# Attention with a feed-forward: float32 loads on the hardware queue and casts on the chip, in place of casting loads from GpSimd's queue

## The chip, the cores and the metric

The kernel runs on one core of a Trainium2 chip. The metric is the device time of one execution in microseconds. The core has a matrix engine (TensorE, PE in the profile; its weight loads are listed apart as PEld), a vector engine (VectorE, DVE), an activation engine (ScalarE, ACT), GpSimd (POOL) and a sequencer that only issues transfers (SyncE, SP). Each works through its own list of instructions in order and waits on semaphores; transfers run on 16 DMA engines.

## What is computed

Windowed attention, followed by a feed-forward layer with a squared ReLU:

```python
# q, k, v: 4 batches, 8 heads, 768 positions, 64 values, float32; n_global = 8, n_local = 96
scores = q @ k.T / sqrt(64)                     # per batch and head
keep = (col < n_global) | ((row - col >= 0) & (row - col < n_local))
dist = where(col < n_global and not local, n_local, abs(row - col))
a = softmax(where(keep, scores - slope[head] * dist, -1e9))
x = (a @ v), heads side by side                 # 3072 x 512
h = maximum(x @ w_in, 0)                        # w_in: 512 x 2048
out = (h * h) @ w_out                           # w_out: 2048 x 512, out float32
```

## The kernel before

**Tiles and stages.** The work is cut into eight half-batches (`hb`, 384 positions each, three blocks of 128). For each, `attention(hb)` makes a list of small jobs over four pairs of heads: `prep` turns q and k of a pair so that the head dimension lies on the partitions, `score` multiplies and applies exp and the mask (two groups), `attend` multiplies with v and divides by the row sums, `to_x` turns the result into `xt`. `ffn(hb)` makes 28 jobs: 16 of `first` (x times w_in, then ReLU and square) and 12 of `second` (times w_out, out). All matrix work is in float16 with float32 sums.

**Order.** TensorE's order is the order in which the jobs are called, fixed by `manual_schedule`. Attention of half-batch 0 stands alone; then `merge` weaves attention of `hb + 1` between the jobs of `ffn(hb)`, about one by one, from the second job on. The other engines' order is made by the framework's scheduler, and each then keeps it.

**Loads.** `load(b, half, h0, h1)` takes the q, k and v tiles of a half-batch, three of 128 positions each. All loads are issued by GpSimd, whose queue also casts float32 in memory to float16 in SBUF. The first half-batch is loaded in two groups of four heads, then come `w_in` in four pieces, half-batch 1, `w_out` in four pieces, half-batch 2, and later half-batches two ahead of use. Outputs go out on SP's queue.

**Around v and k.** A query block looks at its own 128 columns and at the block before. For the block before, copies are kept in which the first 32 rows are replaced by the first 32 of the sequence, where the global columns are: `kb` for k (L172, L173) and `vb` for v (L156 to L159), both made by VectorE. The column of ones that follows v's 64 values gives the row sums.

**Buffers.** `ps_att` (tag `att`) has two PSUM buffers, used in turn by the turned q and k (`trp`), by `av` and by `trx`. `ps_big` has three, used by the scores, by `first` and by `second`. `phat_p` has three of each of its tiles (`ex` and `phat`). `qk_p` has two buffers of q and k turned, `kb`, `v` and `vb`, one for each of two batches.

Of the kernel before, what the change touches and what calls it, by code (L numbers as in the profile page):

```python
# [32 lines left out]
def kernel(  # L33
# [11 lines left out]
    nc = tc.nc  # L45
# [17 lines left out]

    const = ctx.enter_context(tc.tile_pool(name="const", bufs=1))
    stage_p = ctx.enter_context(tc.tile_pool(name="stage", bufs=2))
    qk_p = ctx.enter_context(tc.tile_pool(name="qkp", bufs=2))
    phat_p = ctx.enter_context(tc.tile_pool(name="phat", bufs=3))
    tm_p = ctx.enter_context(tc.tile_pool(name="tm", bufs=3))
    h_p = ctx.enter_context(tc.tile_pool(name="hp", bufs=2))
    y_p = ctx.enter_context(tc.tile_pool(name="yp", bufs=2))  # L70
# [5 lines left out]
    distc = const.tile([P, 2 * P], FP32, name="distc")  # L76
    pidx = const.tile([P, 1], FP32, name="pidx")
    ident = const.tile([P, P], FP16, name="ident")
    local = const.tile([P, 2 * P], FP16, name="local")
    ge0 = const.tile([P, 2 * P], FP16, name="ge0")  # L80
    isg = const.tile([P, 1], FP32, name="isg")
# [9 lines left out]
    def fill_index():  # L91
        nc.gpsimd.iota(dist, pattern=[[1, 2 * P]], base=0, channel_multiplier=-1,
                       allow_small_or_imprecise_dtypes=True)
        nc.gpsimd.iota(pidx, pattern=[[0, 1]], base=0, channel_multiplier=1,
                       allow_small_or_imprecise_dtypes=True)
        nc.vector.tensor_scalar(out=ident, in0=dist[:, 0:P], scalar1=0.0, scalar2=None,
                                op0=ALU.is_equal)

    def fill_masks():
# [30 lines left out]
        bt.sk = [None, None]  # L130
        batches.append(bt)

    def load(b, half, h0, h1):
        bt = batches[b]
        if half == 0 and h0 == 0:
# [5 lines left out]
        if h0 == 0:  # L141
            bt.sq[half] = stage_p.tile([P, HT, H, D], FP16, name="sq", tag="sq")
            bt.sk[half] = stage_p.tile([P, HT, H, D], FP16, name="sk", tag="sk")
        rows = slice(half * HALF, (half + 1) * HALF)
        for src, dst in ((q, bt.sq[half]), (k, bt.sk[half]),
                         (v, bt.v[:, half * HT:(half + 1) * HT, :, 0:D])):
            for t in range(HT):
                r0 = half * HALF + t * P
                nc.gpsimd.dma_start(  # L149
                    out=dst[:, t, h0:h1, :],  # L150
                    in_=src[b, h0:h1, r0:r0 + P, :].rearrange("h p d -> p h d"))

    def fix_v(b, half):
        bt = batches[b]
# [5 lines left out]

    def prep(b, half, a):
        bt = batches[b]
        trp = ps_att.tile([P, 2, HT, P], FP16, name="trp", tag="att")
        for i, st in enumerate((bt.sq[half], bt.sk[half])):
            for t in range(HT):
                nc.tensor.transpose(out=trp[:, i, t, :], in_=st[:, t, 2 * a:2 * a + 2, :],  # L166
                                    identity=ident)
        nc.scalar.copy(out=bt.qk[:, :, a, half * HALF:(half + 1) * HALF],  # L168
                       in_=trp.rearrange("p i t c -> p i (t c)"))
# [143 lines left out]

    fill_index()
    for h0 in range(0, H, 4):
        load(0, 0, h0, h0 + 4)
    fill_masks()
    for c in range(4):
        load_w_in(c)
    load(0, 1, 0, H)  # L320
    for c in range(4):
        load_w_out(c)
    load(1, 0, 0, H)
    with tc.manual_schedule(engines={PE}):
        for job in attention(0):
            job()
        for hb in range(NHB):
            if 1 <= hb and hb + 2 < NHB:
                load((hb + 2) // 2, hb % 2, 0, H)
# [39 lines left out]
```

## Time and profile before

| | before |
|---|---|
| time of the runs (two) | 261.21 and 261.45 us, median 261.33 |
| span of the profiled execution | 258.2 us (its total time is not listed) |
| TensorE busy | 227.6 us, 88% of the span |
| VectorE, ScalarE, GpSimd busy | 139.6, 135.0, 75.9 us |
| GpSimd's queue (casting loads) | 79248 packets, 13.64 MB |
| SP's queue (outputs) | 3328 packets, 6.29 MB |

How to read it: the span runs from the first to the last instruction of the profiled execution; the time of a run lies a little above it. "Busy" is time in which an engine executes, summed over the span. Issuing a load counts as an instruction of GpSimd. A row such as `L272 PE MATMUL hps<-xt,w_in_sb` names the line of the program, the engine, the operation, the tile written and the tiles read. "idle before <-" tells what ended the engine's idle time before that instruction. The megabytes of GpSimd's queue are those written, in float16; twice as many are read.

### The profile page before, as it was taken

The page shows a single profiled execution, that of the slowest core. Times are in us where ns is not written, and L with a number is a line of the kernel's source. Part 1 is how long each engine was busy: PE and PEld are TensorE (multiplying, and loading weights), DVE is VectorE, ACT ScalarE, POOL GpSimd, SP SyncE. Part 2 cuts the span into 40 slices and gives each one's busy share as a digit, 9 for nine tenths or more (in the row PEclk, how much of TensorE's full clock was granted, in tenths as well). Part 3 has the DMA queues.
Part 4 walks back from the last instruction along what each step waited for, and adds up shares of the span by engine and source line. Part 5 has one row for each costly group of instructions (what it writes and reads, how often), then busy time and mean ns, then how long its engine had stood idle before and what let it go on. Part 6 is the DMA issues. An engine that isn't in the chain of part 4 may idle for free.

```text
span 258.2 us, 4590 instructions
## 1 busy us (share of the span) xinstructions
PE 227.6 (88%) x1888; PEld 125.0 (48%) x1888; DVE 139.6 (54%) x331; ACT 135.0 (52%) x201; POOL 75.9 (29%) x95
## 2 busy tenths in 40 slices
PE   1428769928999999999699999999999999999994
PEld 0216345514555555645455555655654565555541
DVE  8558237454778336746676436843675346543411
ACT  5436359601297329941587329831984179623600
POOL 8996573696207000528008000700000000000000
PEclk9999999985999999999999999999999999999999
DMA  6999999999909930499909630792100210003003
GB/s 44 87 116 205 169 179 208 156 153 109 209 1 63 62 121 3 29 96 76 169 3 84 41 122 3 50 76 81 43 0 0 85 41 3 0 5 119 0 3 122
DMA packets 82597, 20.22 MB, mean 78 GB/s; under 512 B 75408, under 2 KB 79504, under 8 KB 82576
## 3 DMA queue, kind: packets, MB, share of 16 engines
q0 software_dynamic: 79248, 13.64, 71.0%
q1 hardware_dynamic: 3328, 6.29, 6.6%
q8 instruction: 15, 0.25, 0.4%
q14 instruction: 6, 0.05, 0.1%
HBM read 27.26 MB, written 6.29 MB: 130 GB/s over the span
## 4 chain that ended last, share of the span: by engine, by line
PE 54%; DMA 17%; ACT 11%; POOL 11%; DVE 3%; issue 2%; DVEq 0%; POOLq 0%
PE yps L284 27%; PE hps L272 19%; DMA v<-in_v_dram 8%; POOL v L149 5%; DMA w_out_sb<-in_moe_w_out_dram 5%; DMA w_in_sb<-in_moe_w_in_dram 5%; ACT hr L276 4%; ACT ex L205 4%; PE av L220 3%; ACT qk L168 3%; PE sp L201 3%; POOL sq L149 2%; POOL sk L149 2%; PE trx L239 1%; POOL w_out_sb L310 1%
## 5 line engine op out<-in xcount | busy, mean ns | idle before, releaser
L272 PE MATMUL hps<-xt,w_in_sb 128*128 128x384 f16 x512 | 98.5, 329 | 2.6 <-DVE y L289 1.9
L276 ACT ACTIVATE hr<-hps 128x768 f16<-128x768 f32 x64 | 52.8, 825 | 43.9 <-PE hps L272 43.0
L272 PEld LDWEIGHTS <-w_in_sb 128*128 128x128 f16 x512 | 45.9, 98 | 31.4 <-issue 3.2
L205 ACT ACTIVATE ex<-sp 128x768 f16<-128x768 f32 x64 | 47.8, 779 | 8.9 <-PE sp L201 8.8
L149 POOL DMA_DIRECT2D sq<-in_q_dram x27 | 23.4, 882 | 71.0 <-PE trp L166 70.5
L206 DVE TENSOR_TENSOR phat<-ex,mask 128x768 f16<-128x768 f16 x64 | 33.0, 523 | 20.5 <-ACT ex L205 17.1
L240 ACT COPY xt<-trx 128x384 f16<-128x384 f16 x32 | 15.3, 478 | 41.1 <-PE trx L239 41.1
L168 ACT COPY qk<-trp 128x768 f16<-128x768 f16 x32 | 25.2, 808 | 15.3 <-PE trp L166 15.3
L289 DVE COPY y<-yps 128x1024 f32<-128x1024 f32 (+1 forms) x16 | 15.3, 958 | 26.3 <-PE yps L284 26.2
L149 POOL DMA_DIRECT2D v<-in_v_dram x27 | 23.3, 883 | 16.3 <-DVE rec L225 8.2
L149 POOL DMA_DIRECT2D sk<-in_k_dram x27 | 23.1, 878 | 4.1 <-DMA w_out_sb<-in_moe_w_out_dram 2.0
L220 PEld LDWEIGHTS <-phat 128*128 128x128 f16 x352 | 15.9, 102 | 16.4 <-DVE tm L227 6.2
L220 PE MATMUL av<-v,phat 128*128 128x65 f16 x192 | 16.4, 201 | 6.8 <-DVE tm L227 5.7
L166 PE MATMUL trp<-ident,sq 128*128 128x128 f16 x96 | 12.4, 229 | 7.4 <-DMA sq<-in_q_dram 7.4
L220 PE MATMUL av<-vb,phat 128*128 128x65 f16 x160 | 15.7, 200 | 3.3 <-DVE vb L157 3.3
L227 DVE TENSOR_TENSOR tm<-av,rec 128x384 f16<-128x384 f32 x32 | 17.8, 556 | 0.9
L201 PE MATMUL sp<-qk 64*128 64x128 f16 x192 | 17.7, 231 | 0.3 <-ACT qk L168 0.3
L201 PE MATMUL sp<-qk,kb 64*128 64x128 f16 x160 | 16.4, 227 | 1.7 <-DVE kb L173 1.7
L166 PE MATMUL trp<-ident,sk 128*128 128x128 f16 x96 | 12.4, 229 | 4.3 <-DMA sk<-in_k_dram 4.2
L172 DVE COPY kb<-qk 128x288 f16<-128x288 f16 (+1 forms) x32 | 10.2, 320 | 9.3 <-ACT qk L168 6.9
L201 PEld LDWEIGHTS <-qk 64*128 64x128 f16 x192 | 8.0, 97 | 14.8 <-issue 12.6
L166 PEld LDWEIGHTS <-sq 128*128 128x128 f16 x96 | 8.3, 101 | 12.3 <-DMA sq<-in_q_dram 8.8
(56 smaller groups left out, 246.6 us busy)
## 6 DMA issues: line engine op xcount, KB each, us to landing
out_dram<-y SPq DMA_DIRECT2D x8, 512.0 KB, 2.8
sq<-in_q_dram POOLq DMA_DIRECT2D x21, 128.0 KB, 5.7
sk<-in_k_dram POOLq DMA_DIRECT2D x21, 128.0 KB, 5.3
v<-in_v_dram POOLq DMA_DIRECT2D x21, 128.0 KB, 6.4
w_in_sb<-in_moe_w_in_dram POOLq DMA_DIRECT2D x4, 512.0 KB, 8.6
w_out_sb<-in_moe_w_out_dram POOLq DMA_DIRECT2D x4, 512.0 KB, 10.5
out_dram<-y SPq DMA_DIRECT2D x8, 256.0 KB, 2.0
sq<-in_q_dram POOLq DMA_DIRECT2D x6, 64.0 KB, 3.0
```

The source lines that it names most:

```text
L149: nc.gpsimd.dma_start(out=dst[:, t, h0:h1, :], in_=src[b, h0:h1, r0:r0 + P, :].rearrange("h p d -> p h d"))
L166: nc.tensor.transpose(out=trp[:, i, t, :], in_=st[:, t, 2 * a:2 * a + 2, :], identity=ident)
L168: nc.scalar.copy(out=bt.qk[:, :, a, half * HALF:(half + 1) * HALF], in_=trp.rearrange("p i t c -> p i (t c)"))
L201: nc.tensor.matmul(sp[:, e, i * P:(i + 1) * P], lhsT=lhsT, rhs=bt.qk[rows, 0, a, r * P:(r + 1) * P], start=True, stop=True)
L205: nc.scalar.activation(out=ex[:, :, 0:n], in_=sp[:, :, 0:n], func=AF.Exp, scale=scale)
L206: nc.vector.tensor_tensor(out=phat[:, :, c0:c0 + n], in0=ex[:, :, 0:n], in1=mask[:, 2 * a:2 * a + 2, m0:m0 + n], op=ALU.mult)
L220: nc.tensor.matmul(av[:, e, j, :], lhsT=phat[:, e, i * P:(i + 1) * P], rhs=bt.vb[:, r - 1, h, :] if before else bt.v[:, r, h, :], start=n ...
L227: nc.vector.tensor_tensor(out=tm.rearrange("p t e d -> p e t d"), in0=av[:, :, :, 0:D], in1=rec[:, :, :, None].to_broadcast([P, 2, HT, D]) ...
L240: nc.scalar.copy(out=xts[hb][:, a, :], in_=trp.rearrange("p t c -> p (t c)"))
L272: nc.tensor.matmul(st["ps"][:, m2, 0:HALF], lhsT=w_in_sb[:, kk, m * P:(m + 1) * P], rhs=xt[:, kk, :], start=kk == 0, stop=kk == NCT - 1)
L276: nc.scalar.activation(out=hr, in_=st["ps"][:, :, 0:HALF], func=AF.Relu)
L284: nc.tensor.matmul(st["y"][:, j % 2, :], lhsT=st["h2"][:, m, j * P:(j + 1) * P], rhs=w_out_sb[:, m, :], start=m == 0, stop=m == NFT - 1)
```

## The change

- All loads go to SP's hardware queue as float32, into new staging tiles (`raw_p`, `wraw_p`, two buffers each), and are cast on the chip: q and v and `w_out` by GpSimd, `w_in` by VectorE.
- k stays float32 in its staging tile. TensorE turns it as float32, with a float32 identity (`ident32`), into a PSUM tile of its own (`trk`); q is turned as before into `trq`. ScalarE makes two copies to SBUF instead of one.
- q is read in rows of three neighbouring positions (`(p t)`), and put back in order by ScalarE's copy, which writes in steps of three.
- `w_in` and `w_out` come in eight pieces each instead of four.
- The first half-batch is no longer loaded in two groups of heads, and `phat_p` has two buffers instead of three.

The diff, cut to its core:

```diff
+    raw_p = ctx.enter_context(tc.tile_pool(name="raw", bufs=2))
+    wraw_p = ctx.enter_context(tc.tile_pool(name="wraw", bufs=2))
-    phat_p = ctx.enter_context(tc.tile_pool(name="phat", bufs=3))
+    phat_p = ctx.enter_context(tc.tile_pool(name="phat", bufs=2))
...
-    def load(b, half, h0, h1):
+    def load(b, half):
...
-            bt.sq[half] = stage_p.tile([P, HT, H, D], FP16, name="sq", tag="sq")
-            bt.sk[half] = stage_p.tile([P, HT, H, D], FP16, name="sk", tag="sk")
+        bt.sq[half] = stage_p.tile([P, HT, H, D], FP16, name="sq", tag="sq")
+        bt.sk[half] = rk = raw_p.tile([P, HT, H, D], FP32, name="rk", tag="rk")
...
-        for src, dst in ((q, bt.sq[half]), (k, bt.sk[half]),
-                         (v, bt.v[:, half * HT:(half + 1) * HT, :, 0:D])):
-            for t in range(HT):
-                r0 = half * HALF + t * P
-                nc.gpsimd.dma_start(
-                    out=dst[:, t, h0:h1, :],
-                    in_=src[b, h0:h1, r0:r0 + P, :].rearrange("h p d -> p h d"))
+        for h0 in range(0, H, H // 2):
+            hs = slice(h0, h0 + H // 2)
+            rq = raw_p.tile([P, H // 2, HT, D], FP32, name="rq", tag="rq")
+            nc.sync.dma_start(
+                out=rq.rearrange("p h t d -> p h (t d)"),
+                in_=q[b, hs, rows, :].rearrange("h (p t) d -> p h (t d)", t=HT))
+            nc.gpsimd.tensor_copy(out=bt.sq[half][:, :, hs, :].rearrange("p t h d -> p h t d"),
+                                  in_=rq)
+        for t in range(HT):
+            r0 = half * HALF + t * P
+            nc.sync.dma_start(out=rk[:, t], in_=k[b, :, r0:r0 + P, :].rearrange("h p d -> p h d"))
+            rv = raw_p.tile([P, H, D], FP32, name="rv", tag="rv")
+            nc.sync.dma_start(out=rv, in_=v[b, :, r0:r0 + P, :].rearrange("h p d -> p h d"))
+            nc.gpsimd.tensor_copy(out=bt.v[:, half * HT + t, :, 0:D], in_=rv)
...
-        trp = ps_att.tile([P, 2, HT, P], FP16, name="trp", tag="att")
-        for i, st in enumerate((bt.sq[half], bt.sk[half])):
-            for t in range(HT):
-                nc.tensor.transpose(out=trp[:, i, t, :], in_=st[:, t, 2 * a:2 * a + 2, :],
-                                    identity=ident)
-        nc.scalar.copy(out=bt.qk[:, :, a, half * HALF:(half + 1) * HALF],
-                       in_=trp.rearrange("p i t c -> p i (t c)"))
+        cols = slice(half * HALF, (half + 1) * HALF)
+        trq = ps_att.tile([P, HT, P], FP16, name="trq", tag="att")
+        for t in range(HT):
+            nc.tensor.transpose(out=trq[:, t, :], in_=bt.sq[half][:, t, 2 * a:2 * a + 2, :],
+                                identity=ident)
+        nc.scalar.copy(out=bt.qk[:, 0, a, cols].rearrange("d (p t) -> d t p", t=HT), in_=trq)
+        trk = ps_att.tile([P, HT, P], FP32, name="trk", tag="att")
+        for t in range(HT):
+            nc.tensor.transpose(out=trk[:, t, :], in_=bt.sk[half][:, t, 2 * a:2 * a + 2, :],
+                                identity=ident32)
+        nc.scalar.copy(out=bt.qk[:, 1, a, cols], in_=trk.rearrange("d t p -> d (t p)"))
...
-        nc.gpsimd.dma_start(
-            out=w_in_sb[:, :, c * n:(c + 1) * n],
-            in_=moe_w_in[:, c * n:(c + 1) * n].rearrange("(k p) f -> p k f", p=P))
+        for kk in range(0, NCT, 2):
+            raw = wraw_p.tile([P, 2, n], FP32, name="wiraw", tag="wraw")
+            nc.sync.dma_start(
+                out=raw, in_=moe_w_in[kk * P:(kk + 2) * P, c * n:(c + 1) * n].rearrange(
+                    "(k p) f -> p k f", p=P))
+            nc.vector.tensor_copy(out=w_in_sb[:, kk:kk + 2, c * n:(c + 1) * n], in_=raw)
...
-        nc.gpsimd.dma_start(
-            out=w_out_sb[:, c * n:(c + 1) * n, :],
-            in_=moe_w_out[c * n * P:(c + 1) * n * P, :].rearrange("(m p) d -> p m d", p=P))
+        for m in range(c * n, (c + 1) * n, 2):
+            raw = wraw_p.tile([P, 2, d_model], FP32, name="woraw", tag="wraw")
+            nc.sync.dma_start(
+                out=raw, in_=moe_w_out[m * P:(m + 2) * P, :].rearrange("(m p) d -> p m d", p=P))
+            nc.gpsimd.tensor_copy(out=w_out_sb[:, m:m + 2, :], in_=raw)
```

More of the change, by code (lines that the diff above doesn't have):

```diff
@@ L78 @@
     ident = const.tile([P, P], FP16, name="ident")
+    ident32 = const.tile([P, P], FP32, name="ident32")
     local = const.tile([P, 2 * P], FP16, name="local")
@@ L96, in fill_index @@
         nc.vector.tensor_scalar(out=ident, in0=dist[:, 0:P], scalar1=0.0, scalar2=None,
+                                op0=ALU.is_equal)
+        nc.vector.tensor_scalar(out=ident32, in0=dist[:, 0:P], scalar1=0.0, scalar2=None,
                                 op0=ALU.is_equal)
@@ L131 @@
         batches.append(bt)
-    def load(b, half, h0, h1):
+    def load(b, half):
         bt = batches[b]
-        if half == 0 and h0 == 0:
+        if half == 0:
             bt.qk = qk_p.tile([P, 2, NPAIR, S], FP16, name="qk", tag="qk")
@@ L303, in load_w_in @@
         n = d_ff // 4
-        nc.gpsimd.dma_start(
-            out=w_in_sb[:, :, c * n:(c + 1) * n],
-            in_=moe_w_in[:, c * n:(c + 1) * n].rearrange("(k p) f -> p k f", p=P))
+        for kk in range(0, NCT, 2):
[4 more added lines that the diff above has]
+            nc.vector.tensor_copy(out=w_in_sb[:, kk:kk + 2, c * n:(c + 1) * n], in_=raw)
     def load_w_out(c):
         n = NFT // 4
-        nc.gpsimd.dma_start(
-            out=w_out_sb[:, c * n:(c + 1) * n, :],
-            in_=moe_w_out[c * n * P:(c + 1) * n * P, :].rearrange("(m p) d -> p m d", p=P))
+        for m in range(c * n, (c + 1) * n, 2):
[3 more added lines that the diff above has]
+            nc.gpsimd.tensor_copy(out=w_out_sb[:, m:m + 2, :], in_=raw)
     fill_index()
-    for h0 in range(0, H, 4):
-        load(0, 0, h0, h0 + 4)
+    load(0, 0)
     fill_masks()
@@ L319 @@
         load_w_in(c)
-    load(0, 1, 0, H)
+    load(0, 1)
     for c in range(4):
         load_w_out(c)
-    load(1, 0, 0, H)
+    load(1, 0)
     with tc.manual_schedule(engines={PE}):
@@ L328 @@
             if 1 <= hb and hb + 2 < NHB:
-                load((hb + 2) // 2, hb % 2, 0, H)
+                load((hb + 2) // 2, hb % 2)
             main = ffn(hb)
```

1 line of the change is left out of this document (removed).

## The prediction

> **What bounds the kernel now.** I read the busy table first, then busy time by stretch (columns: start and end, length, busy us and count for PE, PEld, DVE, ACT, POOL, then granted clock, DMA share, GB/s), then the timeline of TensorE (start, length, engine, line, operation, idle before it).
>
> ```profile
> PE 227.6 (88%) x1888; PEld 125.0 (48%) x1888; DVE 139.6 (54%) x331; ACT 135.0 (52%) x201; POOL 75.9 (29%) x95
> ...
> 0.00:27.00 27.00, 11.89 (x116) 7.48 (x117) 18.47 (x56) 13.26 (x24) 23.16 (x35) 1.00 1.16 118
> 27.00:35.00 8.00, 5.17 (x27) 2.59 (x25) 1.12 (x2) 2.13 (x4) 4.94 (x7) 1.00 2.32 157
> 35.00:53.60 18.60, 18.44 (x180) 9.98 (x178) 9.95 (x22) 14.20 (x20) 11.38 (x13) 1.00 1.79 182
> 53.60:67.20 13.60, 7.94 (x43) 3.96 (x44) 9.04 (x22) 0.96 (x2) 10.09 (x11) 0.75 2.59 129
> 67.20:94.60 27.40, 27.14 (x231) 14.82 (x230) 16.66 (x42) 16.04 (x24) 5.27 (x6) 1.00 0.71 84
> 94.60:121.90 27.30, 27.16 (x244) 15.17 (x243) 16.06 (x35) 16.60 (x24) 9.94 (x12) 1.00 0.66 52
> 121.90:151.70 29.80, 27.42 (x232) 14.91 (x230) 17.44 (x45) 16.27 (x24) 5.83 (x7) 1.00 0.80 87
> ```
>
> Two regimes. From 67.2 us on, one half-batch of feed-forward with the next one's attention woven in takes 27.3 us, of which TensorE is busy 27.2: each nanosecond added to TensorE there lengthens the run, and loads are early. Before 67.2 us TensorE idles 23.8 us (27.0 - 11.9, 8.0 - 5.2, 18.6 - 18.4, 13.6 - 7.9), behind loads.
>
> ```profile
> 27.02 3.88 PE L272 MATMUL hps<-xt,w_in_sb 128*128 128x384 f16 x16
> 34.70 0.23 PE L166 MATMUL trp<-ident,sk 128*128 128x128 f16 x1 [0.64 <-DMA sk<-in_k_dram]
> 46.76 1.02 PE L284 MATMUL yps<-w_out_sb,h_389 128*128 128x512 f16 x4
> 52.53 1.03 PE L284 MATMUL yps<-w_out_sb,h_389 128*128 128x512 f16 x4
> 59.26 0.24 PE L220 MATMUL av<-v,phat 128*128 128x65 f16 x1 [5.71 <-DVE tm L227]
> 59.92 1.90 PE L284 MATMUL yps<-w_out_sb,h_389 128*128 128x512 f16 x4
> 61.92 1.76 PE L284 MATMUL yps<-w_out_sb,h_389 128*128 128x512 f16 x4
> 67.15 1.14 PE L272 MATMUL hps<-xt,w_in_sb 128*128 128x384 f16 x6
> ...
> 54.00 1.76 DVE L159 COPY vb<-v 32x520 f16<-32x520 f16 x5 [5.49 <-DMA v<-in_v_dram]
> ```
>
> The first feed-forward starts at 27.02, the last k tile of half-batch 1 is turned at 34.70, the second product starts at 46.76 and stops at 53.56, because VectorE, which works in order, holds at L159 for v of half-batch 2. After that idle time the clock is down (0.75), so two groups of four matmuls take 1.90 and 1.76 us for 1.03. The next feed-forward starts at 67.15.
>
> **The load path before and after.** GpSimd issues every load, and the queue it feeds is the busiest:
>
> ```profile
> q0 software_dynamic: 79248, 13.64, 71.0%
> ...
> DMA packets 9094, 1.25 MB, mean 157 GB/s; under 512 B 8975, under 2 KB 9094, under 8 KB 9094
> ...
> out_dram<-y SPq DMA_DIRECT2D x8, 512.0 KB, 2.8
> out_dram<-y SPq DMA_DIRECT2D x8, 256.0 KB, 2.0
> ```
>
> The third row is the DMA view of 27 to 35 us: 9094 packets over 16 engines in 8 us are 14.1 ns each, so a k or v tile (1024 packets of 256 B read) drains in 64 x 14.1 = 0.9 us. On the hardware queue two sizes differ by 0.8 us per 256 KB, which leaves 1.2 us fixed; a weight tile of 512 KB then costs 1.6. A k or v tile as float32 is 256 KB in 1024 packets: 0.8 us by bytes, 1.8 if a packet of twice the bytes takes twice the 14.1 ns. I take 1.1, nearer the bytes, since 0.9 already includes reading the full 256 B. Half a q load (384 KB, longer rows) is 1.2.
>
> **First attention.** SP starts about 1.0. Both q halves and k, v, k, v, k follow: 1.0 + 1.2 + 2 x 1.2 + 5 x 1.1 = 10.1 us until the third k tile is there (8.6 to 13.6 by the bounds), where TensorE needs all three for its first pair. Then the changed program's order on VectorE decides: between the first pair's two kb copies stand the rest of the mask, the vb copies and the first two weight casts.
>
> ```profile
> 6.11 0.69 DVE L116 TENSOR_TENSOR mask<-mask,gw 128x1024 f16<-128x1024 f16 x1
> 9.31 0.97 DVE L120 COPY mask<-mask 128x2048 f16<-128x2048 f16 x1
> ...
> L157 DVE COPY vb<-v 64x1560 f16<-64x1560 f16 (+1 forms) x8 | 4.7, 588 | 0.1
> L100 DVE TENSOR_SCALAR distc<-dist 128x256 f32<-128x256 f32 x1 | 0.3, 286 | 0.0
> L289 DVE COPY y<-yps 128x1024 f32<-128x1024 f32 (+1 forms) x16 | 15.3, 958 | 26.3 <-PE yps L284 26.2
> 19.32 0.21 PE L220 MATMUL av<-vb,phat 128*128 128x65 f16 x1 [3.27 <-DVE vb L157]
> ```
>
> A weight cast (128x1024 float32) has no row: 4 x 0.29 = 1.1 us from L100 is the upper end, 0.5 (a quarter of L120's 2048 elements each way) the lower; I take 0.7. From 10.1: turning and two ScalarE copies 1.6, mask 2.4 (L116, its twin L118 and L120), vb 1.1, two casts 1.4, kb 1.0, two phat 0.9: attend of the first pair at 18.5. Now it is at 19.3, and the feed-forward comes 7.7 later; two more casts and the split copies add 1.8, so it starts at 28.0 for 27.0. **About even.**
>
> **Half-batch 1 and w_out.** wraw has two buffers, so a weight load waits for a cast. By the changed order on SP, k tiles 1 and 2 of half-batch 1 stand behind the last two w_in loads, and these behind casts 5 and 6, which VectorE does at the end of the first attention, about 27. Two weight tiles, k, v, k and the fixed part: 3.2 + 3.3 + 1.2 gives 34.7. The tile before came at 34.7 as well: nothing won. The rest of that first product takes 12.0 us now (34.70 to 46.76) plus 2.0 of the next part: second product at 49.0.
> The eight w_out loads queue behind; the first lands about 37, and a GpSimd cast of 1024 elements is priced from
>
> ```profile
> 0.84 0.34 POOL L92 IOTA dist<- 128x256 f32 x1 [0.39 <-POOLq L350]
> ```
>
> as 4 x 0.34 = 1.3 us (it could be 0.7, or 2.7 if a read and write cost double the iota's write alone). Pairs turn in 1.2 + 1.6 + 1.3, about 4.7 with q and k between: the last is cast at 40.1 + 3 x 4.7 = 54.2. TensorE wants it 3.5 us into the second product, 52.5: a wait of 1.7. v of half-batch 2 comes right after, just early enough for the 5.7 us stall at L220 to go. So the next feed-forward starts at 49.0 + 6.8 + 1.7 + 6.3 (67.15 - 59.26 less 1.6 of slow clock) = 63.8, **3.3 us early**.
>
> **The steady part.** Each preparation of a pair now turns k as float32, in its own PSUM tile, with two ScalarE copies instead of one.
>
> ```profile
> 97.03 0.33 PE L166 MATMUL trp<-ident,sq 128*128 128x128 f16 x3
> 97.20 0.33 PE L166 MATMUL trp<-ident,sk 128*128 128x128 f16 x3
> 98.02 0.33 PE L166 MATMUL trp<-ident,sq 128*128 128x128 f16 x3
> 97.23 0.81 ACT L276 ACTIVATE hr<-hps 128x768 f16<-128x768 f32 x1 [0.49 <-PE hps L272]
> 97.94 1.50 ACT L168 COPY qk<-trp 128x768 f16<-128x768 f16 x2
> ...
> L168 ACT COPY qk<-trp 128x768 f16<-128x768 f16 x32 | 25.2, 808 | 15.3 <-PE trp L166 15.3
> L240 ACT COPY xt<-trx 128x384 f16<-128x384 f16 x32 | 15.3, 478 | 41.1 <-PE trx L239 41.1
> L166 PE MATMUL trp<-ident,sk 128*128 128x128 f16 x96 | 12.4, 229 | 4.3 <-DMA sk<-in_k_dram 4.2
> L166 PEld LDWEIGHTS <-sk 128*128 128x128 f16 x96 | 7.3, 101 | 5.8 <-DMA sk<-in_k_dram 5.8
> L227 DVE TENSOR_TENSOR tm<-av,rec 128x384 f16<-128x384 f32 x32 | 17.8, 556 | 0.9
> ```
>
> Three transposes take 97.03 to 97.20, 57 ns each. No row has a float32 one. Lower bound: nothing extra. Upper: load and pass one after the other, 101 + 229 = 330 ns, 273 extra. Twice the bytes at 57 ns each, with part of a 101 ns load exposed, is about 155: I take **0.1 us extra**, 12 x 0.1 = 1.2 per attention.
> The Trainium skill pulls both ways: "TensorE: Matmul & The Clock Gate", Terms, calls transpose mode four times faster for FP32, while "FP8 and Floating Point Precision", TensorE Precision Notes, gives true FP32 four passes. By the first the extra is about nothing, by the second 3 x 57 = 171 ns (estimate), 2.1 us per attention. No run here shows either.
> The pool att still has two buffers, and one preparation now takes both. The second preparation therefore waits until ScalarE has copied both tiles of the first: 98.04 + 2 x 0.48 = 99.0, against its own k at about 98.5: 0.5 us. The fourth waits for tm of the first pair (556 ns, behind a reciprocal): 0.3. ScalarE grows by 2 x 478 - 808 = 0.15 per preparation, beside TensorE's growth, so I add nothing. Together 2.0 per attention, between 0.3 and 4.8. One falls in the start (used above), six after 67 us: **+12.0**.
>
> ```profile
> 125.01 0.56 DVE L156 COPY vb<-v 32x1560 f16<-32x1560 f16 x1 [2.23 <-DMA v<-in_v_dram]
> 126.92 0.81 PE L272 MATMUL hps<-xt,w_in_sb 128*128 128x384 f16 x4 [1.87 <-DVE y L289]
> ```
>
> The 2.4 us that the stretch from 121.9 loses to late v tiles I lower by only 0.5: the third v tile now needs a cast to free its buffer, and y copies stand between. GpSimd's five casts per attention, about 4 us of 27, I cost at nothing: they run a stretch ahead. If that cover is gone, it is the third rival. phat going from three buffers to two costs nothing: each attend comes ahead of the next but one score on TensorE. An output behind a waiting load on SP delays only y, which has two buffers.
>
> **Sum.** 258.2 - 3.3 - 0.5 + 12.0 = 266.4 us of span. The two runs shown (261.21 and 261.45) lie 3.1 above the span; the profiled execution's own total isn't listed. So **269.5 us**.
>
> **Rivals.** First, four passes or an exposed weight load on TensorE: extra 0.2 to 0.27 per transpose, so 12 x 0.1 to 12 x 0.17 more per attention, seven times: 8 to 14 more, 278 to 284. For it: TensorE is busy 227.6 of 258.2 us, so all of it shows; against: the f16 loads hide behind the matmuls.
> Second, other side: **a float32 transpose streams at the f16 pace** (0.057 us, load hidden). Then only the 0.8 us of waits is left per attention: 12.0 becomes 4.8 and the start gains another 1.2, about 261, not slower. It decides from an extra of 0.06 us per transpose downwards. For it: PEld is 48% busy and overlaps; against: four bytes an element.
> Third, GpSimd as the brake: casts at 2.7 instead of 1.3 us put w_out at 8 x 1.4 = 11 later where they are serial, of which TensorE sees about 5: 274.5. In the steady part they delay VectorE.
> The Trainium skill's page "SBUF — State Buffer", Who interferes with whom, says that two-input and two-port VectorE work and GpSimd lock each other out. With VectorE busy 16 of 27.3 us, 4 us of casts would meet some 2.4 us of it, 1 us lost per attention, 276 (estimate). No run here shows it.
> Fourth, the second together with k and v tiles at 0.8 us: the chain of the start gives 4 us more, 255 to 257. That GpSimd still issues loads is out: the changed program's order has none on it.
>
> **Chances.** Forecast 0.42 (own range 264 to 276, three quarters of it above 266.6), first rival 0.17, second 0.21, third 0.10, fourth 0.10. Slower than 2%, what a measurement of this kernel can tell from no change (above 266.6): 0.32 + 0.17 + 0.10 = 0.59. Same: 0.10 + 0.21 = 0.31. Faster (below 256.1): the fourth, 0.10. Range: 258 to 284, leaving out the fourth's better half and the far ends of the first and third.
>
> **What would show it.** Right: a row of trk transposes about 155 ns apart; stretches of 29.3 us where 27.3 stood; the second preparation of each attention waiting on ScalarE; first feed-forward near 28, the next near 64; VectorE casts near 0.7 and GpSimd casts near 1.3 us; no 5.7 us stall at attend. Wrong: stretches still of 27.3 to 28.1 (second rival), of 31 or more (first), or a feed-forward start that moves by over 5 us either way.

## The result, and the profile after

The changed kernel takes **276.34 us** (275.60 and 277.08) against 261.33: 1.058 times as long (95% interval 1.051 to 1.064). Forecast were 269.5 us, with 258 to 284 as the range, and 264 to 276 for the likeliest case by itself. The profiled execution took 275.6 us, its span is 273.8.

Busy time by stretch of the changed kernel, cut at the starts of feed-forwards and of the second product of half-batch 1 (columns: start and end, length, busy us and count of PE, PEld, DVE, ACT, POOL, then granted clock, DMA share, GB/s):

```profile
0.00:31.06 31.06, 12.73 (x117) 8.01 (x118) 21.79 (x63) 15.00 (x28) 7.03 (x13) 1.00 0.88 220
31.06:57.61 26.55, 20.59 (x150) 11.39 (x149) 13.84 (x23) 14.79 (x23) 10.19 (x11) 0.87 0.88 256
57.61:70.90 13.29, 12.68 (x102) 6.26 (x99) 8.58 (x20) 4.23 (x7) 6.26 (x7) 1.00 1.01 237
70.90:249.30 178.40, 169.82 (x1417) 93.93 (x1416) 96.59 (x225) 107.13 (x168) 17.29 (x23) 1.00 0.36 90
249.30:273.80 24.50, 20.93 (x113) 10.87 (x111) 7.07 (x11) 6.48 (x8) 0.00 (x0) 1.00 0.12 45
```

The same view of the kernel before, for its six steady stretches and the rest:

```profile
67.15:233.58 166.43, 163.31 (x1417) 90.20 (x1416) 93.96 (x218) 98.02 (x144) 26.29 (x30) 1.00 0.48 57
233.58:258.20 24.62, 20.92 (x113) 10.87 (x111) 7.08 (x11) 6.48 (x8) 0.00 (x0) 1.00 0.12 45
```

So the 15.6 us of span come from two places: the second feed-forward starts 3.75 us later (70.90 for 67.15), and the six steady stretches take 11.97 us more (178.40 for 166.43). Of the latter, 6.5 us are TensorE's busy time (169.82 for 163.31) and 5.5 its idle time (8.6 for 3.1).

What became of TensorE's idle time in the steady part is in the groups of its instructions from 70.9 to 249.3 us (busy us, mean ns, then idle us before them and what ended it):

```profile
L287 PE MATMUL hps<-xt,w_in_sb 128*128 128x384 f16 x384 | 74.4, 327 | 1.3 <-ACT ex L220 1.3
...
L182 PE MATMUL trk<-ident,rk 128*128 128x128 f32 x72 | 12.4, 281 | 4.7 <-DVE tm L242 4.7
...
L177 PE MATMUL trq<-ident,sq 128*128 128x128 f16 x72 | 7.9, 219 | 2.6 <-ACT qk L179 2.6
```

The three sum to 8.6 us, all of the idle time. The same groups before, from 67.15 to 233.58 us:

```profile
L272 PE MATMUL hps<-xt,w_in_sb 128*128 128x384 f16 x384 | 74.5, 327 | 2.5 <-DVE y L289 1.9
...
L166 PE MATMUL trp<-ident,sq 128*128 128x128 f16 x72 | 7.9, 219 | 0.0
...
L166 PE MATMUL trp<-ident,sk 128*128 128x128 f16 x72 | 7.9, 219 | 0.0
```

Of the 3.1 us of idle time before, 1.9 were one wait for `y`, in the stretch with late v, and 0.6 were waits for `kb`; the transposes waited for nothing. In one attention of the changed kernel (timeline of TensorE) it looks like this:

```profile
103.47 0.33 PE L177 MATMUL trq<-ident,sq 128*128 128x128 f16 x3
103.64 0.50 PE L182 MATMUL trk<-ident,rk 128*128 128x128 f32 x3
105.22 0.33 PE L177 MATMUL trq<-ident,sq 128*128 128x128 f16 x3 [0.43 <-ACT qk L179]
105.54 0.55 PE L182 MATMUL trk<-ident,rk 128*128 128x128 f32 x3
...
111.47 0.81 PE L287 MATMUL hps<-xt,w_in_sb 128*128 128x384 f16 x4 [0.22 <-ACT ex L220]
...
114.26 0.52 PE L182 MATMUL trk<-ident,rk 128*128 128x128 f32 x3 [0.80 <-DVE tm L242]
```

The second preparation waits for ScalarE's copy of the first, the last one for `tm`; each holds the whole in-order engine. The wait at L287 is another one: there a feed-forward matmul waits for ScalarE's exp to free a buffer of `ps_big`. The start, in the same view:

```profile
11.58 0.47 PE L182 MATMUL trk<-ident,rk 128*128 128x128 f32 x1 [1.94 <-DMA rk<-in_k_dram]
...
17.74 0.29 PE L216 MATMUL sp<-qk,kb 64*128 64x128 f16 x2 [3.89 <-DVE kb L188]
...
31.06 5.00 PE L287 MATMUL hps<-xt,w_in_sb 128*128 128x384 f16 x16
...
40.96 0.47 PE L182 MATMUL trk<-ident,rk 128*128 128x128 f32 x1 [1.87 <-DMA rk<-in_k_dram]
...
62.34 0.59 PE L299 MATMUL yps<-w_out_sb,h 128*128 128x512 f16 x2 [0.61 <-POOL w_out_sb L332]
```

And the prices of the new operations, from the groups of all engines:

```profile
L179 ACT COPY qk<-trq 128x384 f16<-128x384 f16 x32 | 25.9, 808 | 3.5 <-PE trq L177 2.9
...
L184 ACT CAST qk<-trk 128x384 f16<-128x384 f32 x32 | 16.5, 515 | 10.7 <-PE trk L182 10.7
L162 POOL CAST v<-rv 128x512 f16<-128x512 f32 x24 | 15.8, 662 | 65.9 <-DMA rv<-in_v_dram 55.8 <-issue 10.1
...
L332 POOL CAST w_out_sb<-woraw 128x1024 f16<-128x1024 f32 x8 | 8.8, 1096 | 8.0 <-DMA woraw<-in_moe_w_out_dram 8.0
L324 DVE CAST w_in_sb<-wiraw 128x1024 f16<-128x1024 f32 x8 | 5.4, 681 | 1.6 <-DMA wiraw<-in_moe_w_in_dram 1.6
```

ScalarE's copy of q, which writes in steps of three, takes 808 ns, where a copy of the same size took 478 before.

### The profile page after: what moved, and what is told of

The parts are those of the page before. It is cut to its first block, busy times and chain, and to the rows that moved or that the text cites. A ratio compares the mean times of both kernels' runs of the same rounds, so it can differ in the third digit from the quotient of the medians.

```text
span 273.8 us, 4724 instructions
## 1 busy us (share of the span) xinstructions
PE 236.7 (86%) x1888; PEld 130.5 (48%) x1888; DVE 147.9 (54%) x340; ACT 147.6 (54%) x233; POOL 40.8 (15%) x54
## 4 chain that ended last, share of the span: by engine, by line
PE 60%; DMA 13%; ACT 10%; DVE 9%; SPq 2%; issue 2%; POOL 2%
PE yps L299 30%; PE hps L287 19%; DMA woraw<-in_moe_w_out_dram 7%; DMA wiraw<-in_moe_w_in_dram 5%; ACT hr L291 4%; PE sp L216 3%; ACT qk L179 3%; PE trk L182 3%; PE av L235 3%; ACT ex L220 2%; DMA rk<-in_k_dram 2%; PE trx L254 2%; DVE phat L221 2%; DVE tm L242 2%; POOL w_out_sb L332 2%
## 5 line engine op out<-in xcount | busy, mean ns | idle before, releaser
L287 PE MATMUL hps<-xt,w_in_sb 128*128 128x384 f16 x512 | 101.2, 336 | 1.5 <-ACT ex L220 1.5
L299 PE MATMUL yps<-w_out_sb,h 128*128 128x512 f16 x384 | 93.6, 379 | 0.6 <-POOL w_out_sb L332 0.6
L287 PEld LDWEIGHTS <-w_in_sb 128*128 128x128 f16 x512 | 48.0, 100 | 32.1 <-issue 4.6
L292 DVE TENSOR_TENSOR h<-hr 128x768 f16<-128x768 f16 x64 | 37.2, 582 | 37.0 <-ACT hr L291 35.2
L299 PEld LDWEIGHTS <-h 128*128 128x128 f16 x384 | 33.8, 98 | 32.6 <-issue 0.9
L255 ACT COPY xt<-trx 128x384 f16<-128x384 f16 x32 | 15.3, 478 | 34.7 <-PE trx L254 34.7
L182 PE MATMUL trk<-ident,rk 128*128 128x128 f32 x96 | 19.3, 307 | 15.7 <-DMA rk<-in_k_dram 8.6
L179 ACT COPY qk<-trq 128x384 f16<-128x384 f16 x32 | 25.9, 808 | 3.5 <-PE trq L177 2.9
L162 POOL CAST v<-rv 128x512 f16<-128x512 f32 x24 | 15.8, 662 | 65.9 <-DMA rv<-in_v_dram 55.8
L155 POOL CAST sq<-rq 128x768 f16<-128x768 f32 x16 | 15.6, 994 | 59.4 <-PE trq L177 35.7
L184 ACT CAST qk<-trk 128x384 f16<-128x384 f32 x32 | 16.5, 515 | 10.7 <-PE trk L182 10.7
L182 PEld LDWEIGHTS trk<-ident,rk 128*128 128x128 f32 x96 | 11.2, 153 | 19.4 <-DMA rk<-in_k_dram 9.1
L235 PEld LDWEIGHTS <-phat 128*128 128x128 f16 x352 | 15.6, 101 | 7.5 <-DVE phat L221 1.9
L177 PE MATMUL trq<-ident,sq 128*128 128x128 f16 x96 | 11.5, 233 | 8.4 <-POOL sq L155 5.8
```

The lines of the kernel that those rows point to most:

```text
L179: nc.scalar.copy(out=bt.qk[:, 0, a, cols].rearrange("d (p t) -> d t p", t=HT), in_=trq)
L182: nc.tensor.transpose(out=trk[:, t, :], in_=bt.sk[half][:, t, 2 * a:2 * a + 2, :], identity=ident32)
L184: nc.scalar.copy(out=bt.qk[:, 1, a, cols], in_=trk.rearrange("d t p -> d (t p)"))
L235: nc.tensor.matmul(av[:, e, j, :], lhsT=phat[:, e, i * P:(i + 1) * P], rhs=bt.vb[:, r - 1, h, :] if before else bt.v[:, r, h, :], start=n ...
L287: nc.tensor.matmul(st["ps"][:, m2, 0:HALF], lhsT=w_in_sb[:, kk, m * P:(m + 1) * P], rhs=xt[:, kk, :], start=kk == 0, stop=kk == NCT - 1)
L292: nc.vector.tensor_tensor(out=st["h2"][:, 2 * i:2 * i + 2, :], in0=hr, in1=hr, op=ALU.mult)
```

## The experiments

Two theories at first: the loss is in the **preparation** (two PSUM tiles, strided copy, float32 transposes), or in the **loads and casts** (bytes, GpSimd against VectorE). Ratios are to the kernel before in the same job, with 95% intervals; "second start" is where the feed-forward of half-batch 1 begins, "six" the length of the six stretches from there, both from the profiled execution.

| kernel | us | ratio | second start | six |
|---|---|---|---|---|
| before | 261.33 | 1 | 67.15 | 166.43 |
| changed | 276.34 | 1.058 (1.051 to 1.064) | 70.90 | 178.40 |
| before, q and k in two tiles | 268.35 | 1.031 (1.027 to 1.034) | 67.63 | 173.87 |
| the same, q strided | 271.26 | 1.043 (1.038 to 1.047) | 68.00 | 176.74 |
| the same, k float32 | 274.93 | 1.057 (1.053 to 1.062) | 68.60 | 180.00 |
| before, one tile, two copies | 262.63 | 1.005 (1.002 to 1.008) | 64.73 | 168.49 |
| changed, weights on the casting queue | 276.22 | 1.060 (1.057 to 1.064) | 72.81 | 177.97 |
| changed, 4 weight buffers | 272.59 | 1.044 (1.038 to 1.050) | 65.98 | 180.64 |
| changed, old preparation | 268.78 | 1.028 (1.021 to 1.036) | 75.39 | 163.79 |
| the same, 4 weight buffers | 256.68 | 0.982 (0.978 to 0.986) | 66.24 | 163.95 |
| the same, q and k of half-batch 0 cast by ScalarE | 255.41 | 0.979 (0.974 to 0.983) | 64.34 | 163.94 |
| before, weights float32 | 274.11 | 1.052 (1.045 to 1.060) | 77.47 | 169.88 |
| before, later loads float32 | 264.12 | 1.010 (1.006 to 1.015) | 70.42 | 165.81 |
| the same, half-batch 0 too | 277.84 | 1.063 (1.058 to 1.067) | 84.42 | 166.46 |

The profiled executions of "one tile, two copies" (259.6 us) and of "old preparation" (265.8) lie 3 us below their medians, so their rows tell where time goes, and their ratios how much. The two kernels with a ratio below 1 are faster than the one before; whether by 2% is open, since both intervals reach across 0.98. "One tile, two copies" and "later loads float32" are slower by 1.5% at most.

### The preparation, step by step

First step: two PSUM tiles, and with them two copies by ScalarE, nothing else (the diffs here are cut to the lines that matter).

```diff
-        trp = ps_att.tile([P, 2, HT, P], FP16, name="trp", tag="att")
+        trq = ps_att.tile([P, HT, P], FP16, name="trq", tag="att")     # q, own copy
+        trk = ps_att.tile([P, HT, P], FP16, name="trk", tag="att")     # k, own copy
...
```

> The kernel before with one edit: q and k of a pair are turned (both float16, both contiguous) into two PSUM tiles and copied by two ScalarE instructions. Theory 'prep' (the steady loss sits in the preparation of a pair): the second preparation of each attention then waits on ScalarE and the fourth on VectorE's tm, together about 0.6 us per attention, 7 attentions, so about 265.5 us. Rival 'casts' (the loss comes from GpSimd casts holding up VectorE, which makes tm late): two tiles alone cost at most 0.2 us per attention, 261.3 to 263.

Second step: q rows read in steps of three and put back by ScalarE.

```diff
...
-        nc.scalar.copy(out=bt.qk[:, 0, a, cols], in_=trq.rearrange("d t p -> d (t p)"))
+        nc.scalar.copy(out=bt.qk[:, 0, a, cols].rearrange("d (p t) -> d t p", t=HT), in_=trq)
```

> As the run before it, and q is read in rows of every third position, so that ScalarE's q copy writes in steps of three. Theory 'prep': that copy takes 0.81 us instead of 0.48 and the waits grow by it, 0.4 us per attention, about 268.5 us. Rival 'casts': ScalarE has room, 262 to 264.

Third step: k loaded as float32 by GpSimd's queue and turned as float32, `phat_p` with two buffers.

```diff
-            bt.sk[half] = stage_p.tile([P, HT, H, D], FP16, name="sk", tag="sk")
+            bt.sk[half] = stage_p.tile([P, HT, H, D], FP32, name="sk", tag="sk")
...
-        trk = ps_att.tile([P, HT, P], FP16, name="trk", tag="att")
+        trk = ps_att.tile([P, HT, P], FP32, name="trk", tag="att")
...
```

> As the run before it, and k is loaded as float32 (still by GpSimd's queue) and turned as float32: the whole preparation of the changed kernel with the loads of the kernel before and no cast on the chip. Theory 'prep': transposes at 110 instead of 57 ns add 0.64 us per attention, stretches of about 29.3 us, about 273 us. Rival 'casts': stretches of 28.2 us at most, 266 to 268, since nothing holds up VectorE.

Measured: 1.031, 1.043, 1.057. With every load still in GpSimd's queue the preparation alone reaches the changed kernel's time. The first step was more than either theory asked for: 265.5 expected, 268.35 measured. The six stretches (busy time by stretch, one row from each of the three kernels, in order):

```profile
67.63:241.50 173.87, 165.50 (x1417) 90.04 (x1416) 93.43 (x218) 100.90 (x168) 26.27 (x30) 1.00 0.46 55
```
```profile
68.00:244.74 176.74, 165.45 (x1418) 90.05 (x1417) 92.58 (x218) 106.08 (x168) 26.43 (x30) 1.00 0.46 54
```
```profile
68.60:248.60 180.00, 169.78 (x1418) 93.94 (x1417) 93.65 (x223) 107.21 (x168) 26.45 (x30) 1.00 0.40 62
```

Splitting adds 7.4 us (from 166.43), 2.2 of them TensorE's busy time; the stride 2.9, none of it busy time of TensorE but 5.2 us of ScalarE's (TensorE's waits for the copy of q grow from 1.4 to 3.0 us, and 2.5 us of waits for exp at the feed-forward appear); float32 3.3, with 4.3 us of busy time.

Is the split dear for ScalarE's second copy, or because a preparation now takes both buffers? One tile, copied by two instructions:

```diff
-        nc.scalar.copy(out=bt.qk[:, :, a, half * HALF:(half + 1) * HALF],
-                       in_=trp.rearrange("p i t c -> p i (t c)"))
+        for i in range(2):
+            nc.scalar.copy(out=bt.qk[:, i, a, half * HALF:(half + 1) * HALF],
+                           in_=trp[:, i].rearrange("p t c -> p (t c)"))
```

> The kernel before with one edit: ScalarE copies the q half and the k half of the same PSUM tile with two instructions (480 ns each) instead of one (808 ns). It adds ScalarE's second copy and leaves the number of PSUM tiles alone. Theory one (the split cost 8 us because a preparation then takes both PSUM buffers): 260 to 262.5. Theory two (it cost 8 us because ScalarE works longer and everything behind it comes later): 266 to 268.5.

Measured: 1.005. The second copy costs about 1.3 us, which leaves the rest of the 8.0 (0.031 x 260.3) to the buffers. The rows of TensorE's groups from 65 to 233 us, first with one tile, then with two:

```profile
L166 PE MATMUL trp<-ident,sq 128*128 128x128 f16 x72 | 7.9, 219 | 0.0
L166 PE MATMUL trp<-ident,sk 128*128 128x128 f16 x72 | 7.9, 219 | 0.0
```
```profile
L171 PE MATMUL trk<-ident,sk 128*128 128x128 f16 x72 | 8.0, 219 | 3.7 <-DVE tm L231 3.4
L166 PE MATMUL trq<-ident,sq 128*128 128x128 f16 x72 | 7.9, 219 | 1.4 <-ACT qk L168 1.4
```

The same transposes wait for nothing in the one and for 5.1 us in the other.

### The loads and the start

Weights back on GpSimd's casting queue, all else as changed:

```diff
-            nc.sync.dma_start(out=raw, in_=moe_w_in[...]); nc.vector.tensor_copy(out=w_in_sb[...], in_=raw)
+        nc.gpsimd.dma_start(out=w_in_sb[:, :, c * n:(c + 1) * n], in_=moe_w_in[...])   # w_out alike
```

> The changed kernel, but w_in and w_out come as before, cast by GpSimd's queue in four pieces each; q, k, v stay on SP's queue with casts on the chip. For the start: theory 'chain' (two staging buffers for weights tie the loads of half-batch 1 and w_out to the casts): the second feed-forward starts near 62 us instead of 70.9, about 267 us. Rival 'bandwidth' (the float32 bytes and small packets fill the DMA engines whatever the order): it starts near 69 us, 274 us or more. The steady stretches stay at 29.7 us in both.

Measured: 276.22, no gain, and not for either reason. The first feed-forward came at 39.37 us. Timelines of GpSimd, VectorE and TensorE:

```profile
20.99 1.48 POOL L324 DMA_DIRECT2D w_out_sb<-in_moe_w_out_dram  x2
33.45 0.62 POOL L161 CAST v<-rv 128x512 f16<-128x512 f32 x1 [10.97 <-DMA rv<-in_v_dram]
36.67 0.62 POOL L161 CAST v<-rv 128x512 f16<-128x512 f32 x1 [1.93 <-DMA rv<-in_v_dram]
```
```profile
37.33 0.42 DVE L166 COPY vb<-v 32x1040 f16<-32x1040 f16 x1 [11.87 <-POOL v L161]
```
```profile
39.08 0.50 PE L253 MATMUL trx<-ident,tm 128*128 128x128 f16 x3 [13.01 <-DVE tm L241]
```

While w_in, and from 21 us w_out, came over the other queue, SP needed 6.4 us each to issue a k tile (from 16.54) and a v tile (from 23.03) of half-batch 1, and GpSimd cast v only at 33.45 and 36.67. VectorE held at `vb` for it, ahead of the last `tm` of half-batch 0. That they held v up fits the kernels with two queues below; this run does not show it by itself. Nor does it test the chain, since moving the weights moved everything. Four buffers leave the order of the queue nearly alone:

```diff
-    wraw_p = ctx.enter_context(tc.tile_pool(name="wraw", bufs=2))
+    wraw_p = ctx.enter_context(tc.tile_pool(name="wraw", bufs=4))
```

> The changed kernel with four weight staging buffers in place of two; nothing else. A weight load then waits for the cast four tiles back, so weight loads bunch together instead of taking turns with the casts. Theory one (the start of the changed kernel is set by the chain load, cast, next load): the last k tile of half-batch 1 comes 3 to 5 us before the 40.96 us of the changed kernel and the next feed-forward starts near 66 in place of 70.9: total 271 to 273. Theory two (the start is set by the float32 bytes, which the queue already moves at 190 to 278 GB/s up to 70 us): 274.5 or more.

Measured: 272.59, second start 65.98, as the chain theory had it (the stretch after it gave 2 us back: 32.2 us long, at a clock of 0.95). The issues of SP, with two buffers and with four (start, length, count):

```profile
16.39 2.44 SPq L321 DMA_DIRECT2D wiraw<-in_moe_w_in_dram  x2
...
22.37 3.25 SPq L321 DMA_DIRECT2D wiraw<-in_moe_w_in_dram  x2
...
30.27 1.43 SPq L321 DMA_DIRECT2D wiraw<-in_moe_w_in_dram  x2
31.75 0.46 SPq L159 DMA_DIRECT2D rk<-in_k_dram  x1
...
32.97 4.45 SPq L159 DMA_DIRECT2D rk<-in_k_dram  x1
```
```profile
9.04 13.18 SPq L321 DMA_DIRECT2D wiraw<-in_moe_w_in_dram  x8
```

With two, the last pair leaves at 30.27 and k of half-batch 1 queues behind it; with four, all eight are out by 22.2.

Now the other half alone: all loads as float32 on the hardware queue, k cast by GpSimd too and q by blocks of 128 like k, the preparation of before.

```diff
-        bt.sk[half] = rk = raw_p.tile([P, HT, H, D], FP32, name="rk", tag="rk")
+        bt.sk[half] = stage_p.tile([P, HT, H, D], FP16, name="sk", tag="sk")
...
+                raw = raw_p.tile([P, H, D], FP32, name=nm, tag=nm)          # q, k, v by blocks of 128
+                nc.sync.dma_start(out=raw, in_=src[b, :, r0:r0 + P, :].rearrange("h p d -> p h d"))
+                nc.gpsimd.tensor_copy(out=dst, in_=raw)
...
```

> The changed kernel with the preparation of the kernel before: k is cast to float16 by GpSimd as v is, q is loaded and cast by blocks of 128 rows as k is, and all six transposes go into one PSUM tile which one ScalarE instruction copies. All loads stay float32 on the hardware queue. GpSimd has nine casts of 128x512 per half-batch. Theory one (the preparation carries the loss, the loads on the hardware queue cost only a few us at the start): stretches of about 27.5 us, total 261 to 266. Theory two (the float32 loads with casts carry it, by GpSimd's lock on VectorE or by the bytes): stretches of 29 us, total 270 or more.

Measured: 268.78, between the two. The stretches are the shortest so far, so theory two falls for the steady part; the second start, 75.39, is the latest so far among the kernels with this loading. With four weight buffers:

> The changed kernel with the old preparation and GpSimd's casts of k (as in the run before it, 268.8 us, whose feed-forward of half-batch 1 starts at 75.39 us) and with four weight staging buffers in place of two. Theory one (two weight buffers make the load wait for the cast, and that sets the start): that feed-forward starts at 69 to 71, as the same four buffers moved it from 70.90 to 65.98 in the changed kernel; total 262 to 264.5. Theory two (GpSimd, which has 18 casts of q, k and v and eight of w_out to do before it, sets the start): 266 or more.

Measured: **256.68 us, faster than the kernel before** (ratio 0.978 to 0.986), more than theory one asked for. Busy time by stretch:

```profile
66.24:230.19 163.95, 163.05 (x1417) 90.16 (x1416) 103.72 (x227) 97.68 (x144) 30.99 (x45) 1.00 0.45 102
```

TensorE idles 0.9 us in six stretches. VectorE is 9.8 us busier than before (103.72 for 93.96) beside 45 casts of GpSimd, and TensorE does not see it. This kernel has `phat_p` with two buffers as well, and they cost its stretches nothing that shows.

Whether the casts cost time in the start was the last question. GpSimd and VectorE of this kernel (timelines):

```profile
4.08 0.61 POOL L151 CAST sq<-rq 128x512 f16<-128x512 f32 x1 [2.82 <-DMA rq<-in_q_dram]
...
7.69 2.41 POOL L151 CAST sq<-rq 128x512 f16<-128x512 f32 x1 [0.59 <-DMA rq<-in_q_dram]
```
```profile
7.34 2.27 DVE L113 TENSOR_TENSOR gw<-far,cg 128x2048 f16<-128x2048 f16 x1
```

The cast begins inside `gw` and ends 0.49 us after it. ScalarE for q and k of half-batch 0:

```diff
-                nc.gpsimd.tensor_copy(out=dst, in_=raw)
+                (nc.gpsimd.tensor_copy if src is v else cast)(out=dst, in_=raw)
...
-    load(0, 0)
+    load(0, 0, nc.scalar.copy)
```

> As the kernel with the old preparation and four weight buffers (256.7 us), but in half-batch 0 ScalarE casts q and k, so that only three casts of v are left to GpSimd before the first feed-forward. There GpSimd's casts of 128x512 take 2.41 and 2.21 us beside VectorE's mask, against 0.61 alone. Theory one (GpSimd and VectorE shut each other out, so the third q and k tiles are late by this): third k tile turned near 13 in place of 15.2 us, first feed-forward near 27.5 in place of 29.05, total 254.5 to 256.5. Theory two (the tiles themselves come late, or what follows is set by the weights): first feed-forward moves by less than 0.5 us, or it moves and the next stays at 66.2; total 256.2 to 257.5.

Measured: 255.41 us. The ratios of the two kernels, 0.979 and 0.982, have overlapping intervals, so the trace has to decide: third k tile turned at 13.18 for 14.96, first feed-forward at 27.68 for 29.05, second at 64.34 for 66.24. That is the course of theory one. How much of it is the two engines shutting each other out, and how much that GpSimd has six casts fewer in its list, this run does not separate.

### Two queues at once

Three kernels kept the casting queue for a part of the loads. Weights as float32 on the hardware queue, the rest of the kernel before:

```diff
+            nc.sync.dma_start(out=raw, in_=moe_w_in[...])           # 4 buffers; w_out alike
+            nc.vector.tensor_copy(out=w_in_sb[...], in_=raw)
...
```

> The kernel before with its weights loaded as float32 by the hardware queue through four staging buffers, w_in cast by VectorE, w_out by GpSimd; q, k and v stay on GpSimd's casting queue, the preparation is that of before. Theory one (the start of before is held by GpSimd, which issues every load in turn): first feed-forward 2 to 4 us earlier, the next near 60 in place of 67, total 253 to 257. Theory two (the DMA engines are shared and already full at the start, or the 32 VectorE and GpSimd casts stand in the way): 260 to 266.

Only the loads inside the loop as float32:

```diff
-                load((hb + 2) // 2, hb % 2, 0, H)
+                load((hb + 2) // 2, hb % 2, 0, H, nc.gpsimd.tensor_copy)     # hardware queue, cast
...
```

> The kernel before; only the loads issued inside the loop (half-batches 3 to 7) come as float32 on the hardware queue and are cast by GpSimd, nine casts of 128x512 each. Preparation, first loads and weights are those of before. Theory one (the hardware queue ends the late v tiles, and casts cost TensorE nothing): start as before, 67.2 us, stretches of 27.0 to 27.5 us as in the changed kernel with the old preparation (163.8 us for six instead of 166.6): 257.5 to 259.5. Theory two (casts take from VectorE what the queue gives): 261 or more.

And those of half-batch 0 too:

```diff
-    for h0 in range(0, H, 4):
-        load(0, 0, h0, h0 + 4)
+    load(0, 0, 0, H, nc.scalar.copy)
```

> As the run before it, and the loads of half-batch 0 too come as float32 on the hardware queue, cast by ScalarE; weights and half-batches 1 and 2 stay on GpSimd's casting queue, which so begins with w_in at 1 us. Theory one (the start is set by GpSimd's queue, which has 15.5 MB of float32 to fetch before the second feed-forward, and this takes 2.4 MB off it): first feed-forward at 23 to 26 us, next at 60 to 64, total 251 to 256. Theory two (the casting queue falls behind while the hardware queue is busy, as when the weights were moved to it and the first feed-forward came at 48.8 us): first feed-forward after 27, total 258 or more.

Measured: 274.11, 264.12 and 277.84: all slower than before, the second by 1%, and most of it in the start (second starts 77.47, 70.42 and 84.42 us for 67.15). The stretches of the second, 165.81 us, are hardly shorter than before, so the gain that theory one had there did not come either. The transfers of the last kernel, issued before 20 us (KB each, median us from issue to landing), above those of k, over the whole run, in the kernel with the old preparation, four weight buffers and everything on the hardware queue:

```profile
rq<-in_q_dram SPq DMA_DIRECT2D x3, 256.0 KB, 3.9
rk<-in_k_dram SPq DMA_DIRECT2D x3, 256.0 KB, 12.2
rv<-in_v_dram SPq DMA_DIRECT2D x2, 256.0 KB, 11.0
sq<-in_q_dram POOLq DMA_DIRECT2D x3, 128.0 KB, 18.8
```
```profile
rk<-in_k_dram SPq DMA_DIRECT2D x24, 256.0 KB, 5.1
```

Beside w_in on the casting queue, a k tile of half-batch 0 takes 12.2 us instead of some 5. The first kernel has it the other way round, w_in on the hardware queue and half-batch 0 on the casting queue. Its pieces of q, issued before 20 us, and those of the kernel before:

```profile
sq<-in_q_dram POOLq DMA_DIRECT2D x6, 64.0 KB, 10.9
```
```profile
sq<-in_q_dram POOLq DMA_DIRECT2D x6, 64.0 KB, 3.0
```

In the second kernel the first tiles of half-batch 3 have free buffers, so they leave at once, and the same pieces of half-batch 0 take 5.5 us. I had counted bytes per queue; the DMA engines are shared, and what is needed first came no sooner than what is needed last.

## Why the prediction was right, and where it was wrong

The direction held (chance 0.59) and the time lies in the range, 6.8 us above the forecast. By its own sum, 258.2 - 3.3 - 0.5 + 12.0 = 266.4, the span should have been 7.4 us shorter than the 273.8 measured.

**"3.3 us early" (start): wrong in sign, 3.75 us late.** This is the step that failed, by 7.1 us, and three parts add up to it.

- The last k of half-batch 1, "34.7", came at 40.96: 6.3 late. The first attention ended later than forecast (feed-forward at 31.06 for 28.0: the third k tile came at 11.58 for 10.1, VectorE did block as described, 3.89 us before 17.74, and the rest of that attention ran longer). The fifth weight cast, done at 30.24, came with it, so the last two w_in loads were issued at 30.27 where I had about 27; then the issue of the last k tile itself took SP 4.45 us (from 32.97). The wait was named rightly, as four buffers show (second start 65.98); its length was too short.
- The rest of that product took 16.65 us where the forecast left 14.3: 2.4 late. Its granted clock was 0.85, after a stretch in which TensorE was busy 5.6 of 9.9 us. I had counted the slow clock after idle time for the kernel before and not for this one.
- The second product took 13.29 us for 14.8: 1.5 early. w_out cost less than forecast (0.61 us for 1.7), and the stall of 5.7 us at attend is gone as said.

**Steady part, -0.5 + 12.0 = 11.5: measured 11.97, but with other shares.** *Float32 transposes:* three take 103.64 to 103.97, 110 ns each for 57 before, not the "about 155". In TensorE's busy time they are 4.3 us over six attentions (third step of the ladder), where I had 7.2. *Waits:* 8.6 us instead of 4.8. The wait for ScalarE in the second preparation came out near its forecast, 2.6 us for 3.0. The wait for `tm` in the fourth was mis-sized: 4.7 for 1.8, and 3.4 already with the split alone. The 1.3 us of waits for exp were not forecast: ScalarE's copies were priced as "2 x 478 - 808 = 0.15 per preparation, so I add nothing". I missed that the q copy writes in steps of three: 808 + 515 - 808 gives 0.5 per preparation, and the strided copy alone is worth 1.2% (1.043 against 1.031). *TensorE busy beside that:* splitting alone made it 2.2 us busier with the same instructions, for which I had nothing. It comes with the waits: after one, the transposes of k begin 0.32 us after those of q (105.22, 105.54), which run out in this time and count as busy, where they begin 0.17 us after them otherwise (103.47, 103.64). That this is all of it is not shown. *Late v tiles, "only 0.5":* nearly all of the 3.1 us of idle time of before went, since no wait for v or y is left in the groups. The errors cancel: 4.3 + 2.2 + 8.6 - 3.1 = 12.0, where I had 7.2 + 4.8 - 0.5 = 11.5. That the two sums agree is luck.

**Outside the span:** 3.1 us assumed, 1.8 measured (275.6 - 273.8).

**Rivals.** *First (four passes):* falls; the extra is 0.053 us per transpose, not 0.2 and more. *Second (f16 pace, deciding "from an extra of 0.06 us per transpose downwards"):* the extra is 0.053 us, so its condition was met, and its time, 261, was not: the two waits that it counted at 0.8 us per attention are 1.2, waits for exp and 2.2 us of busy time came on top, and the start went the other way. The pull of the two pages of the Trainium skill is settled by a row: by "TensorE: Matmul & The Clock Gate", Terms, the extra would be nothing, by "FP8 and Floating Point Precision", TensorE Precision Notes, 171 ns (estimate); measured are 53. *Third (GpSimd as the brake, 274.5 to 276):* the time fits and the cause does not. Casts took 1.1 us for w_out, and the kernel with nine casts per half-batch has the shortest stretches. The Trainium skill's rule, "SBUF — State Buffer", Who interferes with whom, does show in the rows: 2.41 us instead of 0.61 for a cast beside `gw`. Its price shows in the start only and is small: second start 64.34 for 66.24 with six casts on ScalarE, 0.979 against 0.982 in time, with overlapping intervals. *Fourth (tiles at 0.8 us):* falls with 1.2 us per tile; that the chain of the start was the place to win was right, though, and four buffers won it.

**What stays open.** The two halves do not add: the preparation alone is 1.057, the loads alone 1.028, both 1.058. The stretches nearly do: 13.6 longer with the preparation alone, 2.6 shorter with the loads alone, 12.0 longer with both. It is the starts that don't: 1.5 and 8.2 us late, and 3.75 with both. With the old preparation and two weight buffers the second start is 75.39, with the new one 70.90; 4.0 of these 4.5 us come in the second product, where TensorE waits 2.9 us for w_out instead of 0.6 and its granted clock is 0.90. The loads differ there too (q by blocks of 128, nine casts per half-batch on GpSimd for five), and I have not taken these apart; with four weight buffers the two start alike (66.24 and 65.98). Why the wait for `tm` is longer than forecast stays open, and I did not separate `phat_p`'s third buffer from the float32 step.

## What to carry to other kernels

Count buffers before durations: an edit that turns one PSUM tile into two in a pool of two makes later users of that pool wait on an in-order engine, and here that cost more than float32 did on TensorE. Where casts on the chip take turns with loads, the number of staging buffers sets the queue's order, and a cheap second pair (4 KB per partition each) decided whether the same loads lost 7 us or won 5. Test the halves of a compound change apart: here the loads, given two more buffers, were worth some 2%, hidden under the 6% that the preparation cost.

## What the runs showed of the hardware that I had not expected

- A ScalarE copy of 128x384 float16 that writes in steps of three elements takes 808 ns, contiguous 478 to 500.
- Where nothing waits, a float32 transpose of 128x128 follows the last after 110 ns, a float16 one after 57.
- Two DMA queues slow each other, and neither goes first. In the first 20 us of the last kernel with two queues, the hardware queue moved 1.21 MB and the casting queue 2.20 MB (written, so 4.4 MB read), 5.6 MB in all against 4.5 in the kernel with the old preparation, four weight buffers and the hardware queue alone (180 and 270 GB/s there in 0 to 10 and 10 to 20 us). More bytes came, but a k tile's median rose from 5.1 to 12.2 us; with the loads the other way round, a q piece on the casting queue rose from 3.0 to 10.9.
- A GpSimd cast that starts inside a VectorE operation with two inputs took 2.41 us for 0.61 and ended 0.49 us after it, as if it had waited for its end. The other way round as well: in the changed kernel `phat` took 1.27 us for 0.56, begun 0.17 us after a cast of 1.04.
